# Scratch of a weight piece reused two loop steps later, threshold by TENSOR_REDUCE, first queries on ScalarE's queue, first raw weights asked for inside the loop

## The chip, the core and the metric

The kernel runs on one core of a Trainium2 chip. The time is device microseconds of one execution. The three timed runs of the kernel before gave 985.11, 971.95 and 981.6 us, median 981.6. The profile was taken in a further execution of 973.75 us, whose span, from the first to the last instruction, is 972.0 us.

## The reference

Four batches, 576 positions, 8 heads of 64 columns, all in fp32 (the weights come as 64-bit floats). The reference computes, cut to what matters:

```python
scores = scale * q @ k.T                          # per batch and head, 576 x 576
thresh = max(scores, axis=-1) - tau
scores = where(scores >= thresh, scores, -1e9)
attn   = softmax(scores);  x = attn @ v           # heads side by side: 4 x 576 x 512
u  = x + real(fft(fft(x, axis=1), axis=2))        # Fourier mixing over positions and columns
un = (u - mean(u)) / sqrt(var(u) + 1e-6)
x  = u + relu(un @ w_ch1) @ w_ch2                 # 512 -> 2048 -> 512
gate = sigmoid(causal depthwise convolution of x over 5 positions, conv_w)
out  = (gate * (x @ w_val)) @ w_out
```

Each query row keeps only the scores within tau of its maximum.

## The kernel before

The program has one instruction stream for each engine, written out in the order in which Python emits it; no scheduler reorders it. It has two halves.

**The attention loop** (`attention_fft`). The 32 heads are taken in 16 pairs. A pair has 9 score tiles (four 128-row tiles for each head, and one that joins the last 64 rows of both), so there are 144 tiles, two to a loop step: 72 steps and a few more to drain. `ORDER` is a string of atoms that sets what a step emits. `M0`, `M1` (line 570) take the negative row maxima of the two tiles into `neg`, 128x2; `TH` (line 573) makes the threshold `thr` out of them, one instruction of VectorE for both tiles; `E0`, `E1` (line 577) are ScalarE's exponentials, with `neg` as bias; `K0`, `K1` (line 587) mask the exponentials with `thr` and sum them; `C` and `R` make the reciprocal of the sum, `N0`, `N1` (line 594) scale the rows on GpSimd (POOL), `T0`, `T1` transpose them on TensorE, `S2`, `S3` (line 559) are the score products of the next step's tiles. There are two PSUM buffers of scores, so the products of a next tile wait for the mask of a tile before. Between the atoms a filler emits products of probabilities and values (line 304), transposes of the next pair's keys and queries (244 to 263), and the Fourier products (line 228).

Keys, queries and values come by DMAs on SyncE's queue (SP): `load_qk` asks for keys (`kn`, line 186), the last 32 keys and 64 queries (`tn`, 187 and 189) and the other queries (`qn`, 192). Once a batch, a piece of the Fourier stage is written to DRAM in reverse order, element by element, by a DMA on SP (line 356).

**Weight pieces.** The weights come as 64-bit words. 32 pieces of the first two weight matrices, and 8 of the last two, are each converted by a list of instructions in `Wide.stages` (lines 96 to 106): seven or eight on VectorE, ScalarE and, last, POOL. A piece needs a buffer of raw words, filled by a DMA on POOL's queue (`load_raw`, line 866), and one of two pairs of scratch tiles, `cx` and `ct`. In the attention loop the atoms `WD`, `WA` and `WP` each emit at most one instruction of a piece, for VectorE, ScalarE or POOL. `tick` runs at the end of each step: it counts the step, stores the high and low half of a finished piece to DRAM (`e_h<-cx`, `e_l<-ct`, line 919, on SP), puts its scratch pair on the list `stored` with the step from which it may be taken again (the present one and `STORE` more, here 0), and asks for new raw words. The first instruction of a piece (line 96) writes `cx`, and so waits on the chip until the store that last read this scratch has landed. In the loop 18 pieces are converted.

**The second half** (`mlp`, `gate_out`): the drain of the attention, norms, the two large products (lines 1054 and 1070), the gate and the last two products. It begins with DMAs that fetch the stored pieces (line 849, first at 426.8 us).

Of the kernel before, what the change touches and what calls it, by code (L numbers as in the profile page):

```python
# [11 lines left out]
F32 = mybir.dt.float32  # L12
# [3 lines left out]
AF = mybir.ActivationFunctionType  # L16
ALU = mybir.AluOpType
AX = mybir.AxisListType
# [3 lines left out]
B, H, S, D = 4, 8, 576, 64  # L22
# [4 lines left out]
MAIN, TAIL = 512, 64  # L27
HALF = S // 2
# [12 lines left out]
SPLITS = 6  # L41
KEYS_ACT = False
CYCLE = 'wfgssvgwnsfhtc'
STORE = 0
SPENT = 2
EARLY = 18
QORD = (1, 0, 4, 2, 3)
# [8 lines left out]
def f32(ap):  # L56
    return ap.bitcast(F32)
# [77 lines left out]
def attention_fft(tc, right, ps_f, a, u_d, dram, conv_w, hooks):  # L135
    nc = tc.nc
    PE, DVE, ACT, POOL, SP = nc.tensor, nc.vector, nc.scalar, nc.gpsimd, nc.sync
    left, right1 = ExitStack(), ExitStack()
    with ExitStack() as right2, ExitStack() as right2b, ExitStack() as right3, ExitStack() as right4, ExitStack() as scores, ExitStack() as turned:
        def pool(stack, name, bufs, side="right", **kw):  # L140
            return stack.enter_context(tc.tile_pool(name=name, bufs=bufs, side=side, **kw))
# [3 lines left out]
        const = pool(right1, "const", 1)  # L145
        x_p = pool(right1, "x", XB)
        sm_p = pool(right1, "sm", 6)
# [10 lines left out]

        ident = id_p.tile([128, 128], F32, name="ident")
        tau = const.tile([128, 1], F32, name="tau_sb")  # L160
        ntau = const.tile([128, 1], F32, name="ntau")
        alpha = const.tile([128, 1], F32, name="alpha")
        cst = {}
        POOL.dma_start(out=tau, in_=a["tau"].to_broadcast([128, 1]))
        hooks["begin"]()
        DVE.memset(alpha, 0.0)
        ACT.activation(ntau, alpha, AF.Exp)

        vs = [(const.tile([128, 2, 4, D], F32, name=f"v{i}"), const.tile([128, 2, D], F32, name=f"vt{i}")) for i in range(2)]
        ths = [[const.tile([128, 2, n], F32, name=f"th{i}_{n}") for n in (256, 320)] for i in range(2)]  # L170
# [5 lines left out]
        NPAIR = B * NP  # L176
        nat = {}

        def load_qk(p):
            b, hs = p // NP, slice(2 * (p % NP), 2 * (p % NP) + 2)  # L180
            kn = nat_p.tile([128, 2, 2, 2, D], F32, tag="kn", name="kn")
            qn = nat_p.tile([128, 2, 4, 2, D], F32, tag="qn", name="qn")
            tn = nat_p.tile([96, 2, 2, D], F32, tag="tn", name="tn")
            k, q = a["k"][b, hs].rearrange("h (g p) d -> p h g d", g=2), a["q"][b, hs]
            for j in range(2):
                SP.dma_start(out=kn[:, j], in_=k[j * 128:j * 128 + 128])
            SP.dma_start(out=tn[0:32], in_=k[256:HALF])
            for j in range(2):
                SP.dma_start(out=tn[32:96, :, j], in_=q[:, MAIN:S].rearrange("h p d -> p h d"))
            for h in range(2):  # L190
                for j in range(2):
                    SP.dma_start(out=qn[:, h, :, j], in_=q[h, 0:MAIN].rearrange("(t p) d -> p t d", p=128))
            nat[p] = tn, kn, qn

        def load_v(p):
# [37 lines left out]
        def g_prep_qk(p):  # L233
# [33 lines left out]
            if 0 < p < NPAIR - 1:  # L267
                load_qk(p + 1)
# [271 lines left out]
        sc, neg, thr, ex, ssum, prob = {}, {}, {}, {}, {}, {}  # L540
# [24 lines left out]

        def emit_max(g):
            if g % 2 == 0:
                neg[g // 2], thr[g // 2], ssum[g // 2] = (sm_p.tile([128, 2], F32, tag=nm, name=nm) for nm in ("neg", "thr", "su"))
            i, j = divmod(g, 2)
            DVE.tensor_reduce(out=neg[i][:, j:j + 1], in_=sc[g][:, :, 0:HALF], axis=AX.XY, op=ALU.max, negate=True)  # L570

        def emit_thr(i):
            DVE.tensor_scalar(out=thr[i], in0=neg[i], scalar1=-1.0, scalar2=ntau[:, 0:1], op0=ALU.mult, op1=ALU.add)

        def emit_exp(g):
            e = e_p.tile([128, 2, HALF], F32, tag="e", name="e")
            ACT.activation(e, sc[g][:, :, 0:HALF], AF.Exp, bias=neg[g // 2][:, g % 2:g % 2 + 1], scale=1.0)  # L577
            ex[g] = e

        def emit_mask(g):  # L580
# [38 lines left out]
        def emit_t(g):  # L619
# [20 lines left out]
            if h == 2:  # L640
                q_tail.append(g_tail(p, c, [p_t[p, i][:, MAIN:S]], th[0:64, :, 256:320], (i,)))

        LAG = 4
        SP.dma_start(out=ident, in_=a["ident"])
        load_qk(0)
        DVE.tensor_scalar(out=ntau, in0=tau, scalar1=-1.0, scalar2=None, op0=ALU.mult)
        DVE.tensor_tensor(out=ntau, in0=ntau, in1=tau, op=ALU.min)
        DVE.tensor_scalar(out=alpha, in0=tau, scalar1=0.0, scalar2=float(D) ** -0.5,
                          op0=ALU.is_ge, op1=ALU.mult)
        q_prep.append(g_prep_qk(0))  # L650
        while q_prep:
            fill(1e9)
            flush()
        load_qk(1)
        emit_s(0)
        emit_s(1)
# [8 lines left out]
        for u in range(NT // 2 + 3):  # L665
            t = 2 * u
            on = [x for x in (t, t + 1) if x < NT]
            state["tile"] = t
            for x in on:
                p, h, i = tiles[x]  # L670
# [7 lines left out]
            on2 = bool(on)  # L678
# [3 lines left out]
            def M0():  # L682
                if on2: emit_max(t)
            def M1():
                if on2: emit_max(t + 1)
            def TH():
                if on2: emit_thr(u)
            def E0():
                if on2: emit_exp(t)
# [21 lines left out]
                if t + 3 < NT: emit_s(t + 3)  # L711
            def C():
                if on2: ACT.activation(ssum[u], ssum[u], AF.Copy, bias=1e-9)
            def TA():
                if on2: ACT.activation(thr[u], neg[u], AF.Identity, scale=-1.0, bias=ntau[:, 0:1])
            def TP():
                if on2: POOL.tensor_scalar(out=thr[u], in0=neg[u], scalar1=-1.0, scalar2=ntau[:, 0:1], op0=ALU.mult, op1=ALU.add)
            def CP():
                if on2: POOL.tensor_scalar(out=ssum[u], in0=ssum[u], scalar1=1e-9, scalar2=0.0, op0=ALU.add, op1=ALU.add)
            def Q():  # L720
# [22 lines left out]
            for atom in ORDER.split():  # L743
                env[atom]()
            tq.clear()
            hooks["tick"]()
            if left and NPAIR - 1 in kq:
                left.close()
# [33 lines left out]
def mlp(tc, right, ps_f, attention, hooks, a, u_d, y_d, dram, wide, cw, out):  # L782
    nc = tc.nc
    PE, DVE, ACT, POOL, SP = nc.tensor, nc.vector, nc.scalar, nc.gpsimd, nc.sync
# [6 lines left out]
    with ExitStack() as ctx, ExitStack() as top, ExitStack() as top2:  # L791
# [16 lines left out]
        active, outbox, stored = deque(), [], deque()  # L808
        at, loaded, clock = [0], [0], [0]
# [19 lines left out]
        def give(slot):  # L829

            if nxt[0] < FB:
                nxt[0] += 1
                assign(nxt[0] - 1, slot)
            else:
                assign(gone.pop(0), slot)
# [10 lines left out]
        def place(k):  # L846
            j, i = pieces[k][1]
            for t, d in zip(w[j][i], e_d[k]):
                SP.dma_start(out=f32(t), in_=d)
            placed.add(k)  # L850
# [56 lines left out]
        def tick():  # L907

            clock[0] += 1
            while spent and spent[0][0] <= clock[0]:  # L910
                nxt[1] -= 1
                give(spent.popleft()[1])
            while stored and stored[0][0] <= clock[0]:
                spare["cv"].append(stored.popleft()[1])
            for k, room, dst in outbox:
                j, i = pieces[k][1]
                if isinstance(j, str) or k < EARLY:
                    for t, d in zip(dst, e_d[k] if k < EARLY else [d[i * 128:(i + 1) * 128] for d in w_d[j]]):
                        SP.dma_start(out=d, in_=f32(t))
                    written.add(k)  # L920
                    if k in wanted:
                        place(k)
                else:
                    placed.add(k)
                stored.append((clock[0] + STORE, room))
                spare["raw"].append(raws.pop(k)[0])
            outbox.clear()
            load_raw()
# [188 lines left out]
        tail = None  # L1117
# [413 lines left out]
```

## Time and profile before

| | |
|---|---|
| timed runs | 985.11, 971.95, 981.6 us (median 981.6) |
| profiled execution | 973.75 us, span 972.0 us, mean granted TensorE clock 0.978 |
| PE (TensorE products) | busy 894.6 us, 92% |
| DVE (VectorE) | busy 580.0 us, 60% |
| ACT (ScalarE) | busy 454.2 us, 47% |
| POOL (GpSimd) | busy 368.0 us, 38% |

Shares over the whole span mix two halves: up to about 425 us TensorE and VectorE are both busy most of the time and wait for each other; from about 450 us on TensorE is busy all of it but for a stretch around 525 to 545 us. A row of the timeline gives the start, the duration, the engine, the line and the instruction; what stands in square brackets is how long the engine had been idle before it, and what ended that. An engine name with a q (SPq) is the queue on which a DMA is issued, and the duration is that of issuing it.

### The profile page before, as it was taken

What the parts mean: (1) busy time and instruction counts of PE and PEld (TensorE: products, weight loads), DVE (VectorE), ACT (ScalarE), POOL (GpSimd) and SP (SyncE); (2) the same over time, 40 slices, a digit from 0 to 9 for tenths busy, and PEclk for the clock granted to TensorE, in tenths of its full rate; (3) what the DMA queues carried; (4) which work ended last, traced back from release to release, by engine and by line L of the source; (5) the groups of instructions that cost most, each with busy time, mean ns of one, the idle gap of its engine ahead of it and who ended that gap; (6) DMA issues with size and microseconds to landing.
All of it is one profiled execution on the core that took longest, in us unless ns stands there. A gap on an engine that the chain in (4) does not pass through costs nothing. (4 is left out here: it accounts for less than half of the span.)

```text
span 972.0 us, 14884 instructions
## 1 busy us (share of the span) xinstructions
PE 894.6 (92%) x5232; PEld 712.3 (73%) x5232; DVE 580.0 (60%) x1228; ACT 454.2 (47%) x915; POOL 368.0 (38%) x450
## 2 busy tenths in 40 slices
PE   4888986898979999979997999999999999999998
PEld 2555564555756566648885899999999989998897
DVE  4998876787968677732569534444222256734750
ACT  3767764666767676643545423322312213214432
POOL 2475542476627634561455412321031011028421
PEclk9999897998999999999999999999999999999999
DMA  7686441465637442257637922421230022143211
GB/s 182 155 198 155 137 118 66 141 171 168 166 111 203 131 108 80 78 186 286 232 112 250 345 107 87 135 69 42 71 114 1 1 88 86 44 143 109 102 44 66
DMA packets 136227, 123.61 MB, mean 127 GB/s; under 512 B 86630, under 2 KB 100182, under 8 KB 136152
## 3 DMA queue, kind: packets, MB, share of 16 engines
q1 hardware_dynamic: 129160, 98.16, 33.0%
q0 software_dynamic: 6992, 24.49, 8.4%
q8 instruction: 42, 0.69, 0.3%
q14 instruction: 33, 0.27, 0.1%
HBM read 90.11 MB, written 37.22 MB: 131 GB/s over the span
## 5 line engine op out<-in xcount | busy, mean ns | idle before, releaser
L1058 DVE SCALAR_TENSOR_TENSOR hl<-h,hh 128x448 fp32r<-128x448 f32 (+1 forms) x80 | 50.9, 637 | 203.5 <-ACT hh L1057 203.5
L1057 ACT ACTIVATE hh<-h 128x448 fp32r<-128x448 f32 (+1 forms) x80 | 44.4, 555 | 257.7 <-PE h L1054 257.7
L594 POOL TENSOR_SCALAR p<-p,su 128x576 f32<-128x576 f32 x144 | 109.1, 763 | 125.1 <-DVE su L681 103.9
L559 PE MATMUL s<-kt,qt 64*128 64x288 f32 (+1 forms) x640 | 105.9, 467 | 30.2 <-DVE p L587 30.0
L587 DVE SCALAR_TENSOR_TENSOR p<-s,thr,e 128x576 f32<-128x576 f32 x144 | 112.5, 815 | 34.0 <-ACT e L577 16.3
L1070 PE MATMUL c<-hl,w1h 128*128 128x448 f32 (+1 forms) x320 | 118.9, 371 | 0.5 <-DVE hl L1058 0.5
L1070 PE MATMUL c<-hh,w1h 128*128 128x448 f32 (+1 forms) x320 | 119.0, 372 | 0.0
L1070 PE MATMUL c<-hh,w1l 128*128 128x448 f32 (+1 forms) x320 | 118.7, 371 | 0.0
L577 ACT ACTIVATE e<-s,neg 128x576 f32<-128x576 f32 x144 | 99.4, 736 | 41.2 <-DVE neg L570 41.0
L570 DVE TENSOR_REDUCE neg<-s 128x1 f32<-128x576 f32 x144 | 101.7, 745 | 15.5 <-PE s L559 15.2
L559 PEld LDWEIGHTS s<-kt,qt 64*128 64x128 f32 (+1 forms) x640 | 47.2, 184 | 74.4 <-DVE p L587 27.9
L637 ACT ACTIVATE m<-t 128x512 f32<-128x512 f32 x144 | 84.5, 587 | 7.7 <-PE t L628 7.7
L1054 PE MATMUL h<-unh,w0h 128*128 128x448 f32 (+1 forms) x320 | 80.2, 372 | 5.4 <-DMA w0h<-e_h 3.2
L1054 PE MATMUL h<-unh,w0l 128*128 128x448 f32 (+1 forms) x320 | 80.9, 375 | 4.2 <-POOL w0l L106 4.2
L628 PE MATMUL t<-ident,p 128*128 128x128 f32 x576 | 79.3, 281 | 3.7 <-POOL xf L334 1.9
L304 PE MATMUL f<-m,v 128*64 128x320 f32 (+1 forms) x512 | 80.4, 415 | 1.7 <-ACT m L637 1.2
L1054 PE MATMUL h<-unl,w0h 128*128 128x448 f32 (+1 forms) x320 | 80.7, 374 | 0.0
L628 PEld LDWEIGHTS t<-ident,p 128*128 128x128 f32 x576 | 65.4, 143 | 19.7 <-issue 9.9
L1054 PEld LDWEIGHTS h<-unh,w0h 128*128 128x128 f32 x320 | 59.9, 188 | 13.4 <-DMA w0h<-e_h 3.8
L1054 PEld LDWEIGHTS h<-unh,w0l 128*128 128x128 f32 x320 | 60.1, 189 | 12.1 <-POOL w0l L106 5.5
L1054 PEld LDWEIGHTS h<-unl,w0h 128*128 128x128 f32 x320 | 60.7, 190 | 7.0
L1070 PEld LDWEIGHTS c<-hl,w1h 128*128 128x128 f32 x320 | 60.1, 188 | 7.7 <-DVE hl L1058 0.8
(218 smaller groups left out, 1574.5 us busy)
## 6 DMA issues: line engine op xcount, KB each, us to landing
raw<-in_moe_w_ch POOLq DMA_DIRECT2D x32, 512.0 KB, 5.5
qn<-in_q SPq DMA_DIRECT2D x64, 128.0 KB
e_h<-cx SPq DMA_DIRECT2D x18, 256.0 KB
e_l<-ct SPq DMA_DIRECT2D x18, 256.0 KB
xs<-xt SPq DMA_DIRECT2D x16, 288.0 KB
w0h<-e_h SPq DMA_DIRECT2D x18, 256.0 KB
w0l<-e_l SPq DMA_DIRECT2D x18, 256.0 KB
w1h<-e_h SPq DMA_DIRECT2D x18, 256.0 KB
```

What stands on the lines that cost most here:

```text
L304: PE.matmul(out=f[h * 64:h * 64 + 64, 0:n], lhsT=w, rhs=r, start=(t == 0), stop=(t == 4))
L559: PE.matmul(out=s[o, c, 0:HALF], lhsT=qt[w, hh, q], rhs=kt[w, hh, :], start=True, stop=True)
L570: DVE.tensor_reduce(out=neg[i][:, j:j + 1], in_=sc[g][:, :, 0:HALF], axis=AX.XY, op=ALU.max, negate=True)
L577: ACT.activation(e, sc[g][:, :, 0:HALF], AF.Exp, bias=neg[g // 2][:, g % 2:g % 2 + 1], scale=1.0)
L587: DVE.scalar_tensor_tensor(out=p_view(g).rearrange("p (a b) -> p a b", a=2), in0=sc.pop(g)[:, :, 0:HALF], scalar=thr[g // 2][:, j], in1=ex ...
L594: POOL.tensor_scalar(out=v, in0=v, scalar1=su, scalar2=1.0, op0=ALU.mult, op1=ALU.mult)
L628: PE.matmul(out=f[:, t, :], lhsT=pv[:, t * 128:(t + 1) * 128], rhs=ident, is_transpose=True, start=(t == 0), stop=(t == 3))
L637: tq.append(lambda: ACT.activation(o, fv, AF.Copy))
L1054: PE.matmul(out=f[:, 0:n], lhsT=ww[:, k * 128:(k + 1) * 128], rhs=x[:, k, 0:n], start=(i == 0), stop=(i == 3 * KB - 1))
L1057: ACT.activation(hh, f[:, 0:n], AF.Relu)
L1058: DVE.scalar_tensor_tensor(out=hl, in0=f[:, 0:n], scalar=0.0, in1=f32(hh), op0=ALU.max, op1=ALU.subtract)
L1070: PE.matmul(out=ch[c][o][:, 0:n], lhsT=ww[:, o * 128:(o + 1) * 128], rhs=x, start=(at_ == 0 and i == 0), stop=(at_ == FB - 1 and i == 2))
```

## The change

Four things. The scratch of a finished piece goes back on the list with `STORE = 2`, so that the next piece may take it two loop steps later; in the second half it stays 0. The threshold is one TENSOR_REDUCE with negation over pairs (negative maximum, `atau`), in six fixed tiles `neg0` to `neg5` whose second column is filled with `atau`, the larger of tau and minus tau, by twelve copies at the start; before it was one TENSOR_SCALAR. The load of tau, and the query loads of the first pair, are issued by ScalarE instead of POOL and SP. And the call that first asks for raw weights is taken from the start of the kernel and put at the end of the second loop step.

```diff
-STORE = 0
+STORE = 2
...
-        ntau = const.tile([128, 1], F32, name="ntau")
+        atau = const.tile([128, 1], F32, name="atau")
...
-        POOL.dma_start(out=tau, in_=a["tau"].to_broadcast([128, 1]))
-        hooks["begin"]()
+        negs = [const.tile([128, 2, 2], F32, name=f"neg{i}") for i in range(6)]
+        ACT.dma_start(out=tau, in_=a["tau"].to_broadcast([128, 1]))
         DVE.memset(alpha, 0.0)
-        ACT.activation(ntau, alpha, AF.Exp)
+        ACT.activation(atau, alpha, AF.Exp)
...
-        def load_qk(p):
+        def load_qk(p, second=SP):
...
-                SP.dma_start(out=tn[32:96, :, j], in_=q[:, MAIN:S].rearrange("h p d -> p h d"))
+                second.dma_start(out=tn[32:96, :, j], in_=q[:, MAIN:S].rearrange("h p d -> p h d"))
...
-                    SP.dma_start(out=qn[:, h, :, j], in_=q[h, 0:MAIN].rearrange("(t p) d -> p t d", p=128))
+                    second.dma_start(out=qn[:, h, :, j], in_=q[h, 0:MAIN].rearrange("(t p) d -> p t d", p=128))
...
-            DVE.tensor_reduce(out=neg[i][:, j:j + 1], in_=sc[g][:, :, 0:HALF], axis=AX.XY, op=ALU.max, negate=True)
+            DVE.tensor_reduce(out=neg[i][:, j, 0:1], in_=sc[g][:, :, 0:HALF], axis=AX.XY, op=ALU.max, negate=True)
 
         def emit_thr(i):
-            DVE.tensor_scalar(out=thr[i], in0=neg[i], scalar1=-1.0, scalar2=ntau[:, 0:1], op0=ALU.mult, op1=ALU.add)
+            DVE.tensor_reduce(out=thr[i], in_=neg[i], axis=AX.X, op=ALU.add, negate=True)
...
-        load_qk(0)
-        DVE.tensor_scalar(out=ntau, in0=tau, scalar1=-1.0, scalar2=None, op0=ALU.mult)
-        DVE.tensor_tensor(out=ntau, in0=ntau, in1=tau, op=ALU.min)
+        load_qk(0, ACT)
+        DVE.tensor_scalar(out=atau, in0=tau, scalar1=-1.0, scalar2=None, op0=ALU.mult)
+        DVE.tensor_tensor(out=atau, in0=atau, in1=tau, op=ALU.max)
+        for t in negs:
+            for j in range(2):
+                DVE.tensor_copy(t[:, j, 1:2], atau)
...
             tq.clear()
+            if u == 1:
+                hooks["begin"]()
             hooks["tick"]()
...
-                stored.append((clock[0] + STORE, room))
+                stored.append((clock[0] + (STORE if tail is None else 0), room))
```

`hooks["begin"]` is `load_raw`, which `tick` calls too, at its own end. TensorE's order stays the same, row for row; so does every engine's order from the end of the attention loop on. What moves in the loop is the pieces. On VectorE, at the place where the first batch's Fourier products begin (step 24; `ael` and `aeh` are parts of their result, `su` the row sums), the kernel before has the end of one piece (101, 102) and straight behind it the first instruction of another (96):

```order
L389 TENSOR_TENSOR ael<-f,aeh 97x258 [waits Activation_49]
L101 SCALAR_TENSOR_TENSOR raw<-raw,ct 128x512
L102 TENSOR_SCALAR raw<-cx 128x512
L96 TENSOR_SCALAR cx<-raw 128x512 [waits DMAHW2_49,DMASW1_49]
L681 RECIPROCAL su<-su 128x2 [waits Activation_49]
L570 TENSOR_REDUCE neg<-s 128x1 [waits PE_49] x2
L389 TENSOR_TENSOR ael<-f,aeh 96x258 [waits Activation_49]
L573 TENSOR_SCALAR thr<-neg,ntau 128x2 [waits DVE_49]
```

In the changed kernel the same place has the middle of a piece (100), and the first instruction of the next one a step later:

```order
L389 TENSOR_TENSOR ael<-f,aeh 97x258 [waits Activation_49]
L100 SCALAR_TENSOR_TENSOR cx<-raw,cx 128x512
L685 RECIPROCAL su<-su 128x2 [waits Activation_49]
L571 TENSOR_REDUCE neg_189<-s 128x1 [waits PE_49] x2
L389 TENSOR_TENSOR ael<-f,aeh 96x258 [waits Activation_49]
L574 TENSOR_REDUCE thr<-neg_189 128x2 [waits DVE_49]
L588 SCALAR_TENSOR_TENSOR p,su<-s,thr,e 128x576 [waits DVE_49,Activation_49]
L588 SCALAR_TENSOR_TENSOR p,su<-s,thr,e 128x576 [waits Activation_49,Pool_49]
L389 TENSOR_TENSOR ael<-f,aeh 96x258 [waits Activation_49]
L101 SCALAR_TENSOR_TENSOR raw<-raw,ct 128x512
L102 TENSOR_SCALAR raw<-cx 128x512
L96 TENSOR_SCALAR cx<-raw 128x512 [waits DMAHW6_49,DMASW7_49]
```

From here on the changed kernel begins a piece every third step, and the last instructions of the eighteenth (101, 102) stand in step 58 of 72; before, in step 51, with up to six instructions of pieces in one step on VectorE and none in others. The scratch that a piece takes was stored about three steps before.

The other place is the start. On POOL's queue the kernel before has tau, then three loads of raw words, then the first row scaling:

```order
L164 DMA tau_sb_185<-in_tau 128x1
L866 DMA raw_189<-in_moe_w_ch1 128x4x256
L866 DMA raw_191<-in_moe_w_ch2 128x1024
L866 DMA raw_193<-in_moe_w_ch1 128x4x256
L594 ISA
L594 TENSOR_SCALAR p_292<-p_292,su_274 128x576 [waits DVE_49]
```

In the changed kernel:

```order
L868 DMA raw_326<-in_moe_w_ch1 128x4x256
L868 DMA raw_328<-in_moe_w_ch2 128x1024
L868 DMA raw_330<-in_moe_w_ch1 128x4x256
L595 ISA
L595 TENSOR_SCALAR p_303<-p_303,su_285 128x576 [waits DVE_49]
```

The three loads still stand ahead of everything else that POOL does, and none of them waits for anything; only tau is gone. ScalarE's stream of the changed kernel begins with tau, the table load, and the six query loads, of which the last three wait for earlier DMAs (`DMAHW4_49` is the semaphore of the first of the two `tn` loads in front of them):

```order
L165 DMA tau_sb<-in_tau 128x1
L167 ACT_TABLE_LOAD
L167 ACTIVATE atau<-alpha 128x1 [waits DVE_49]
L189 DMA tn<-in_q 64x2x64 x2
L192 DMA qn<-in_q 128x4x64
L192 DMA qn<-in_q 128x4x64 [waits DMAHW0_49]
L192 DMA qn<-in_q 128x4x64 [waits DMAHW2_49]
L192 DMA qn<-in_q 128x4x64 [waits DMAHW4_49]
L257 ACTIVATE qt<-f,alpha 128x2x64 [waits DVE_49,PE_49]
```

Before, that stream went from the table load and one ACTIVATE straight to line 257, and the six loads stood on SP behind `ident`, two `kn` and one `tn`.

## Rows read from the trace of the kernel before

**Rows 1.** Page, part 1: busy us, share of the span, instructions.
```profile
PE 894.6 (92%) x5232; PEld 712.3 (73%) x5232; DVE 580.0 (60%) x1228; ACT 454.2 (47%) x915; POOL 368.0 (38%) x450
```

**Rows 2.** Windows: stretch, its length, busy of each engine, TensorE clock, DMA share, GB/s.
```profile
150.00:175.00 25.00, 17.15 (x117) 12.66 (x119) 20.04 (x47) 14.88 (x32) 7.54 (x10) 0.84 0.19 59
...
200.00:225.00 25.00, 23.93 (x163) 14.17 (x160) 20.96 (x45) 15.28 (x32) 18.92 (x24) 1.00 0.75 198
```

**Rows 3.** Waits, all engines: who waited for whom, us in total, times, longest.
```profile
PE s L559 <- DVE p L587: 30.0, 29, 3.0
...
DVE cx L96 <- DMA e_h<-cx: 16.8, 3, 10.9
DVE p L587 <- ACT e L577: 16.3, 18, 2.3
```

**Rows 4.** Timeline, step 24: reversal, piece's store, VectorE's and TensorE's idle time.
```profile
133.01 0.69 SPq L356 DMA_DIRECT2D xr<-xs  x1
...
133.81 9.59 SPq L919 DMA_DIRECT2D e_h<-cx  x1
...
151.54 0.43 DVE L96 TENSOR_SCALAR cx<-raw 128x512 int32<-128x512 int32 x1 [10.95 <-DMA e_h<-cx]
...
153.75 1.17 PE L228 MATMUL f<-sdh,xoh 128*96 128x256 f32 x4 [9.69 <-DVE ael L389]
```

**Rows 5.** Timeline, 262 to 286 us: the second such wait.
```profile
273.37 0.43 DVE L96 TENSOR_SCALAR cx<-raw 128x512 int32<-128x512 int32 x1 [4.46 <-DMA e_h<-cx]
...
275.57 0.39 PE L254 MATMUL f<-ident,tn 96*128 96x96 f32 x2 [3.36 <-DVE bol L389]
```

**Rows 6.** Lines of VectorE, 0 to 440 us: count, busy us, mean ns, idle before.
```profile
L573 DVE TENSOR_SCALAR thr<-neg,ntau 128x2 f32<-128x2 f32 x72 | 31.5, 438 | 2.0
...
L97 DVE TENSOR_SCALAR ct<-raw 128x512 int32<-128x512 int32 x18 | 12.1, 671 | 0.0
```

**Rows 7.** Single lines: count, duration ns least/median/most, first and last start.
```profile
L573 DVE TENSOR_SCALAR thr<-neg,ntau x72: 216/266/1906, 16.7 to 419.2; 128x2 f32<-128x2 f32 x72
...
L570 DVE TENSOR_REDUCE neg<-s x144: 725/746/760, 15.0 to 418.4; 128x1 f32<-128x576 f32 x144
...
L681 DVE RECIPROCAL su<-su x72: 145/157/171, 19.3 to 423.6; 128x2 f32<-128x2 f32 x72
...
L97 DVE TENSOR_SCALAR ct<-raw x40: 406/420/3497, 36.0 to 664.6; 128x512 int32<-128x512 int32 x40
```

**Rows 8.** Timeline, step 24: a long threshold beside POOL, and who waits.
```profile
135.74 1.91 DVE L573 TENSOR_SCALAR thr<-neg,ntau 128x2 f32<-128x2 f32 x1
136.16 1.47 POOL L594 TENSOR_SCALAR p<-p,su 128x576 f32<-128x576 f32 x2
...
138.63 1.49 PE L559 MATMUL s<-kt,qt 64*128 64x288 f32 x8 [1.41 <-DVE p L587]
```

**Rows 9.** Timeline, first 16 us: loads, and TensorE's and VectorE's first waits.
```profile
0.74 1.28 ACT L167 ACT_TABLE_LOAD   x1 [0.74 <-PEq L1520]
...
1.24 0.74 POOL L164 DMA_DIRECT2D tau_sb<-in_tau  x1 [0.80 <-POOLq L1520]
...
1.97 2.05 POOL L866 DMA_DIRECT2D raw<-in_moe_w_ch  x3
...
2.74 1.39 SPq L189 DMA_DIRECT2D tn<-in_q  x2
...
4.18 2.61 SPq L192 DMA_DIRECT2D qn<-in_q  x4
...
10.43 0.56 PE L254 MATMUL f<-ident,tn 96*128 96x96 f32 x2 [4.41 <-DMA tn<-in_q]
...
14.98 0.76 DVE L570 TENSOR_REDUCE neg<-s 128x1 f32<-128x576 f32 x1 [3.33 <-PE s L559]
```

**Rows 10.** Tile e_h: stores and later fetches, count, duration ns, first and last start.
```profile
L919 SPq DMA_DIRECT2D e_h<-cx x18: 319/430/9591, 45.5 to 312.4; - x18
L849 SPq DMA_DIRECT2D w0h<-e_h x18: 319/320/9483, 426.8 to 547.1; - x18
```

More of the change, by code (lines that the diff above doesn't have):

```diff
@@ L567, in emit_max @@
             if g % 2 == 0:
-                neg[g // 2], thr[g // 2], ssum[g // 2] = (sm_p.tile([128, 2], F32, tag=nm, name=nm) for nm in ("neg", "thr", "su"))
+                thr[g // 2], ssum[g // 2] = (sm_p.tile([128, 2], F32, tag=nm, name=nm) for nm in ("thr", "su"))
+            neg[g // 2] = negs[g // 2 % len(negs)]
             i, j = divmod(g, 2)
-            DVE.tensor_reduce(out=neg[i][:, j:j + 1], in_=sc[g][:, :, 0:HALF], axis=AX.XY, op=ALU.max, negate=True)
+            DVE.tensor_reduce(out=neg[i][:, j, 0:1], in_=sc[g][:, :, 0:HALF], axis=AX.XY, op=ALU.max, negate=True)
         def emit_thr(i):
-            DVE.tensor_scalar(out=thr[i], in0=neg[i], scalar1=-1.0, scalar2=ntau[:, 0:1], op0=ALU.mult, op1=ALU.add)
+            DVE.tensor_reduce(out=thr[i], in_=neg[i], axis=AX.X, op=ALU.add, negate=True)
         def emit_exp(g):
             e = e_p.tile([128, 2, HALF], F32, tag="e", name="e")
-            ACT.activation(e, sc[g][:, :, 0:HALF], AF.Exp, bias=neg[g // 2][:, g % 2:g % 2 + 1], scale=1.0)
+            ACT.activation(e, sc[g][:, :, 0:HALF], AF.Exp, bias=neg[g // 2][:, g % 2, 0:1], scale=1.0)
             ex[g] = e
@@ L713, in C @@
                 if on2: ACT.activation(ssum[u], ssum[u], AF.Copy, bias=1e-9)
[L714 to L717, printed above, removed]
             def CP():
```

## The prediction

> **What bounds the kernel now.** I read the page's shares first [rows 1]. TensorE's 92% says little, since it mixes two halves; so next the windows of 25 us. In the second half TensorE works without a break, and the change leaves every engine's order there as it is. The attention loop is another matter: from 200 to 225 us TensorE is busy 23.93 us and VectorE 20.96; from 150 to 175 us TensorE has only 17.15 at a granted clock of 0.84, VectorE 20.04 [rows 2]. Both are nearly full and wait for each other, by the two score buffers: products, maxima, threshold, masks, next products. Any time by which the masks come sooner can move the loop, and any stop of VectorE stops TensorE a little later.
>
> Then the waits [rows 3]. The products of a next tile waited 30.0 us, 29 times, for a mask. VectorE waited 16.8 us, in three pieces of up to 10.9, for the store of a piece's high half: it stood at the first instruction of a piece (line 96), whose scratch was still being read, with maxima and masks queued behind. Last the places. At step 24 the reversal goes out on SP at 133.01; the store behind it takes 9.59 us to issue, and VectorE starts again at 151.54, idle for 10.95 us; TensorE starts at 153.75 after 9.69 idle [rows 4]. At 273.37 the same costs VectorE 4.46 and TensorE 3.36 [rows 5]. The third piece of the wait, 16.8 less these two, is 1.4 us.
>
> The other loss is line 573, the threshold. Its 72 instructions take 31.5 us, 438 ns in the mean [rows 6], but the shortest takes 216 ns and the longest 1906 [rows 7]. At 135.74 it lasts 1.91 us and ends when POOL's two row scalings end (136.16 + 1.47 = 137.63); TensorE then waits 1.41 us for the mask [rows 8]. An instruction on 128x2 numbers has no work for that: it is held while POOL works.
>
> **The scratch.** A step takes (419.2 - 16.7) / 71 = 5.67 us, from the first and last threshold [rows 7], so two steps are 11.3 us. The longest wait is 10.95, so the added distance covers each of the three. At step 24 there is also no first instruction of a piece behind the reversal any more: it stands a step later, on scratch stored about three steps before, 17.0 us, against 151.54 - 133.81 = 17.7 from that store's issue to VectorE's release in the worst case [rows 4]. I take the two gaps of TensorE, 9.69 + 3.36 = 13.0 us, as the gain. Ends: nothing, if another wait ends as late; 16.8 us, all that VectorE stood.
>
> What that costs: each piece comes later, the last in step 58 instead of 51. Seven steps are 40 us; the last store now goes out at 312.4, then at about 352, and the first fetch comes at 426.8 [rows 10]. Hidden by 74 us; without that margin the excess would come in full. Instructions of pieces stay the same in number, about 90 on VectorE, and lie more evenly: nothing for that.
>
> **The threshold.** Held time is 31.5 - 72 x 0.216 = 15.9 us. How much of it reaches the end? In 18 steps the mask waited for the exponentials anyway, 16.3 us in all [rows 3], and there a shorter threshold is worth nothing; where it lasted longest, TensorE lost 1.41 of the 1.69 us above the shortest [rows 8]. So at most 54 of 72 steps times 83%, 62%; I take half, 8 us, if TENSOR_REDUCE isn't held. Does a row say so? The 144 maxima, the same operation, stay between 725 and 760 ns, but read PSUM; the reciprocals of 128x2, SBUF to SBUF, between 145 and 171; TENSOR_SCALAR from SBUF goes to 3497 ns (line 97) [rows 7]. That is for it, not proof. The Trainium skill (SBUF — State Buffer, section "SBUF: two separate sides") says that VectorE and GpSimd lock one shared pair of ports against each other for a whole instruction, and that VectorE needs it for two-port modes or two SBUF inputs; the Trainium skill's page VectorE: DVE Perf Modes, section "The perf-mode tier table", gives tensor_reduce no two-port mode. By that rule it is never held; the trace agrees on who is held, and no run here shows the new instruction.
>
> Its own length: the nearest row in size is the reciprocal of 128x2, median 157 ns. From above: the maximum's 745 ns for 576 numbers, shrunk as TENSOR_SCALAR shrinks from 128x512 to 128x2 (least 406 to 216 ns [rows 7]), is 0.40 us. I take 157, since four numbers are nearest to two: 72 x 0.059 = 4.2 us less on VectorE, half of it on the path, 2 us. At 0.40 it costs 72 x 0.184 = 13.2 us and eats nearly all of the 15.9.
>
> **The start.** The diff says that raw words are asked for later. The order says that they are not: nothing stands ahead of the three loads on POOL, and they wait for nothing, so they go out when POOL starts, at 1.24 instead of 1.97, with tau's 0.74 us gone [rows 9]. What held the first queries back should thus stay: they were issued from 2.74 on, and TensorE got them at 10.43, having waited 4.41 us. ScalarE can't issue them sooner than SP did: behind tau stands its table load, 0.74 to 2.02. Issuing takes ScalarE 1.39 + 2.61 = 4.0 us [rows 9], at a time when it has nothing else to do; were it busy, 4.0 us. The twelve copies, 12 x 0.157 = 1.9 us, lie in a VectorE that later idles 3.33 us for the first scores. I take 0. Ends: a gain of 4.41, the whole wait; a loss where the last query load waits for the first `tn`, as its semaphore now says: issued at 10.43 and landing as `tn` did, 7.69 us after its issue, it is there at 18.1, and the first maximum, with 1.49 us for the products [rows 8], starts at 19.6 instead of 14.98, 4.6 later.
>
> **Sum.** 13 + 8 + 2 + 0 = 23 us, against the profiled execution of 973.75: 951 us. That execution lies 7.85 us under the median of 981.6, and the three runs span 13 us. I put the median two thirds of that distance above the sum: **956 us**.
>
> **Rivals.**
> 1. TENSOR_REDUCE is held or slow as well, and only the scratch gains. For it: no row has this operation on SBUF operands alone; against it the reciprocals. 973.75 - 13 = 961, median 966. The Trainium skill speaks for this too: its page VectorE: DVE Perf Modes, section "Rules for kernel authors", calls tensor_reduce on a hot path VectorE's slowest operation, at 1×; at twice the 216 ns the sum would lose 72 x 0.216 = 15.6 us of VectorE's 15.9, and come to the same 961. The row on the maxima fits 1×, but here there are four elements. Chance 0.13.
> 2. The wait for a store comes back: a piece now begins every third step whatever the queue does, and a store that goes out behind a reversal needs 17.7 us against 17.0. Only the threshold's 10 us are left: 964, median 969. Against it: at step 24 no such instruction stands there any more. Chance 0.13.
> 3. The raw words do come later after all: the 4.41 us at the start are gained as well. 947, median 952. Against it the order. Chance 0.05.
> 4. Slower: the time for which POOL holds VectorE moves to the pieces' own instructions, which now stand singly in nearly every step beside the row scalings. Line 97 already takes 671 ns in the mean, 265 above its least [rows 6, 7]. If each of 90 instructions waited for one scaling, 0.73 us, that is 66 us on VectorE, half of it, 33, on the path: 973.75 - 23 + 33 = 984, median 989. It decides from 0.51 us on each, twice what line 97 has. Chance 0.05.
> 5. TensorE fills the time: its gaps come back elsewhere, the sum stays within 5 us of 974. Chance 0.07.
>
> The forecast, with both gains between half and full, has 0.57: 938 to 965.
>
> **Range and chances.** About 2% is what a measurement of this kernel can tell from no change; 2% below 981.6 is 962. The range runs from 938 (16.8, 15.9 and 4.2 us in full, 973.75 - 37, with little added) to 974, which takes in rivals 1 to 3. Faster by over 2%: three quarters of the forecast, rival 3 and a little of 1 and 2, 0.54. Slower by over 2%, beyond 1001, needs more than rival 4 at its price: 0.04. Within 2%: 0.42.
>
> **What will show it.** Line 96 has no wait for `e_h`, and TensorE no gap above 5 us between 130 and 160 us. The threshold's 72 rows lie near 160 ns, the longest under 250, about 12 us in all. TensorE's wait for masks falls from 30.0 to under 20 us. Raw loads stand at about 1.2 us, and the first maximum within 4 us of 14.98. The first fetch of a stored piece moves from 426.8 to about 404, and everything behind it by as much. I am wrong if the threshold still spreads to above 1 us, if line 96 still waits, or if both are as forecast and 426.8 hardly moves.

## The result, and the profile after

The changed kernel takes 943.96 us in the median (940.76 to 945.86) against 980.86 in runs of the kernel before beside it: a ratio of 0.963, 95% interval 0.956 to 0.971. On a second chip it took 943.1 against 976.0, ratio 0.967 (0.964 to 0.969). The prediction of 956 us, with a range of 938 to 974, called it faster; it fell 12 us short of the gain. The profiled execution took 940.76 us, span 939.0.

The page's first part, busy us, share and instructions, answers [rows 1]:

```profile
PE 882.5 (94%) x5232; PEld 705.2 (75%) x5232; DVE 561.6 (60%) x1240; ACT 453.0 (48%) x915; POOL 365.0 (39%) x449
```

TensorE does the same 5232 products in 12.1 us less busy time. That is the first thing that the prediction had no term for. The windows of 25 us [rows 2] show where:

```profile
150.00:175.00 25.00, 23.20 (x174) 15.57 (x172) 20.77 (x51) 19.73 (x44) 13.65 (x20) 1.00 0.56 160
200.00:225.00 25.00, 23.41 (x176) 14.63 (x176) 21.46 (x51) 20.15 (x44) 15.35 (x22) 1.00 0.63 181
```

The stretch that had 17.15 us of TensorE at a granted clock of 0.84 has 23.20 at 1.00. Over the whole loop, from the first threshold to the last, the same view of the kernel before and, after it, of the changed kernel on the second chip:

```profile
17.00:419.00 402.00, 352.79 (x2478) 231.78 (x2476) 319.51 (x730) 270.14 (x572) 209.89 (x280) 0.95 0.50 137
```
```profile
17.00:388.00 371.00, 341.90 (x2479) 226.94 (x2477) 304.09 (x731) 268.73 (x572) 206.38 (x280) 0.99 0.54 148
```

31 us go. 10.9 of them are TensorE's busy time, at a mean granted clock of 0.99 instead of 0.95; 20.1 are its idle time. I sorted that idle time by the length of the gaps between one product's end and the next one's start: gaps above 2 us fall from 23.5 us in six places to 2.5 in one, and those of 0.5 to 2 us stay (22.9 and 24.1 us). So the gain is long stops and what follows them, not a little from every step. The waits say the same [rows 3]. First a line of that view of the kernel before which is not among those rows, then the changed kernel's:

```profile
ACT e L577 <- DVE neg L570: 41.0, 29, 10.6
```
```profile
PE s L559 <- DVE p L588: 27.1, 29, 2.5
ACT e L578 <- DVE neg L571: 25.8, 23, 2.9
DVE p L588 <- ACT e L578: 14.4, 24, 1.3
```

TensorE's many short waits for masks hardly change (30.0 before); ScalarE's waits for the maxima lose 15.2 us, and the one of 10.6 is gone. No wait of line 96 for a store is left. The reversal and the store behind it still go out, and that store still takes 7.67 us to issue; nothing on VectorE waits for it, and the next piece begins at 137.73 without a wait [rows 4]:

```profile
131.05 0.69 SPq L356 DMA_DIRECT2D xr<-xs  x1
...
132.29 7.67 SPq L921 DMA_DIRECT2D e_h<-cx  x1
...
137.73 0.42 DVE L96 TENSOR_SCALAR cx<-raw 128x512 int32<-128x512 int32 x1
```

The single lines [rows 7], duration least/median/most in ns:

```profile
L574 DVE TENSOR_REDUCE thr<-neg x72: 141/157/159, 17.0 to 385.5; 128x2 f32<-128x4 f32 x72
...
L571 DVE TENSOR_REDUCE neg<-s x144: 730/747/759, 15.5 to 384.7; 128x1 f32<-128x576 f32 x144
...
L97 DVE TENSOR_SCALAR ct<-raw x40: 408/422/4112, 39.7 to 631.4; 128x512 int32<-128x512 int32 x40
```

The new threshold is never held. Line 97 still is, and now more: 921 ns in the mean over the loop, before 671 [rows 6]:

```profile
L97 DVE TENSOR_SCALAR ct<-raw 128x512 int32<-128x512 int32 x18 | 16.6, 921 | 0.0
```

The start [rows 9]:

```profile
1.26 2.26 POOL L868 DMA_DIRECT2D raw<-in_moe_w_ch  x3 [0.81 <-POOLq L1522]
...
1.43 1.32 ACTq L189 DMA_DIRECT2D tn<-in_q  x2
...
10.50 0.90 PE L244 MATMUL f<-ident,kn 128*128 128x128 f32 x3 [5.25 <-DMA kn<-in_k]
...
15.54 1.42 DVE L571 TENSOR_REDUCE neg<-s 128x1 f32<-128x576 f32 x2 [2.63 <-PE s L559]
```

The raw loads go out at 1.26, as the order said. The queries are no longer what TensorE waits for; now it is the second half of the keys, at 10.50. The first maximum starts 0.56 us later than before.

The fetches of the stored pieces [rows 10] begin 33.5 us earlier, and what is behind them keeps that distance to within 1 us:

```profile
L921 SPq DMA_DIRECT2D e_h<-cx x18: 376/422/7932, 51.9 to 315.4; - x18
L851 SPq DMA_DIRECT2D w0h<-e_h x18: 319/320/9062, 393.3 to 513.3; - x18
```

### The profile page after: what moved, and what is told of

Its sections match the earlier page's. It is cut to its first block, busy times and chain, and to the rows that moved or that the text cites. A ratio compares the mean times of both kernels' runs of the same rounds, so it can differ in the third digit from the quotient of the medians.

```text
span 939.0 us, 14896 instructions
## 1 busy us (share of the span) xinstructions
PE 882.5 (94%) x5232; PEld 705.2 (75%) x5232; DVE 561.6 (60%) x1240; ACT 453.0 (48%) x915; POOL 365.0 (39%) x449
## 5 line engine op out<-in xcount | busy, mean ns | idle before, releaser
L559 PE MATMUL s<-kt,qt 64*128 64x288 f32 (+1 forms) x640 | 99.6, 441 | 27.1 <-DVE p L588 27.1
L559 PEld LDWEIGHTS s<-kt,qt 64*128 64x128 f32 (+1 forms) x640 | 45.2, 175 | 69.0 <-issue 27.8
L1056 PEld LDWEIGHTS h<-unh,w0h 128*128 128x128 f32 x320 | 60.1, 189 | 11.4 <-ACT w0h L105 3.0
L106 POOL TENSOR_TENSOR ct<-raw 128x512 fp32r<-128x512 f32 x26 | 28.8, 1113 | 99.5 <-DVE raw L102 55.0
## 6 DMA issues: line engine op xcount, KB each, us to landing
w0h<-e_h SPq DMA_DIRECT2D x18, 256.0 KB, 16.1
```

The costliest lines, as they stand in the source:

```text
L559: PE.matmul(out=s[o, c, 0:HALF], lhsT=qt[w, hh, q], rhs=kt[w, hh, :], start=True, stop=True)
L1056: PE.matmul(out=f[:, 0:n], lhsT=ww[:, k * 128:(k + 1) * 128], rhs=x[:, k, 0:n], start=(i == 0), stop=(i == 3 * KB - 1))
```

## The experiments

**Theory A**: the gain is the two terms of the prediction, each enlarged by what follows a stop of VectorE: TensorE stands, its granted clock falls, and the next products are slower. **Rival B**: the terms are only mis-sized (the stops' own length, the threshold's held time in full). Each kernel was timed over five rounds beside the kernel before; gains are given in per cent of it (1% is 9.8 us), with 95% intervals. Experiments 1 to 4 ran on one chip; 6, 9, 10 and the changed kernel on a second; 5, 7, 8 and 11 on a third. Across chips, "by the ratios" compares the gains over the kernel before, "by the medians" the times as they are.

**1. Without the scratch's distance.**

```diff
-STORE = 2
+STORE = 0
```

> The changed kernel with STORE = 0, all else as changed: a finished piece's scratch is free for the next piece at once, so line 96 should stand behind the store again. Theory A (what the long stops cost is TensorE's idle time and also the lower granted clock behind them; the scratch is worth about 24 us, 16 of stops and 8 of slower products): 943.96 + 24 = 968 us, line 96 waits about 17 us for stores, TensorE's granted clock in the loop falls below 0.97 in the stretches behind the stops. Rival B (the scratch is worth its stops alone, as predicted, and the threshold nearly all its held time): 943.96 + 14 = 958 us.

961.7 us, a gain of 1.6% (1.3 to 1.9) instead of the changed kernel's 3.3: the distance is worth 1.7%, 16.7 us. The wait is back, but shorter than before, 6.02 us, because in this kernel the pieces begin a step later than in the kernel before; TensorE then waits 4.94 us:

```profile
151.27 0.43 DVE L96 TENSOR_SCALAR cx<-raw 128x512 int32<-128x512 int32 x1 [6.02 <-DMA e_h<-cx]
...
153.47 1.06 PE L609 MATMUL f<-ident,p 128*64 128x128 f32 x4 [4.94 <-DVE thr L574]
```

A's 24 us is out. Rival B's 14 lies at the edge of the interval (13 to 20 us), but the wait is only a third of the one that B priced, so something beside the stop seems to be in it (experiment 5).

**2. Without TENSOR_REDUCE.**

```diff
-            DVE.tensor_reduce(out=thr[i], in_=neg[i], axis=AX.X, op=ALU.add, negate=True)
+            DVE.tensor_scalar(out=thr[i], in0=neg[i][:, :, 0], scalar1=-1.0, scalar2=atau[:, 0:1], op0=ALU.mult, op1=ALU.subtract)
```

> The changed kernel with the threshold by TENSOR_SCALAR as before (negated and less atau, out of the same six tiles), all else as changed. Theory A: the threshold is worth about 10 us as predicted: 954 us; its 72 rows take about 31 us again, the longest near 1.9 us. Rival B (threshold in VectorE's chain is worth nearly all of its 20 us, and more by the clock): 964 us. Rival C (TENSOR_REDUCE's gain is given back elsewhere, the scratch is all of it): 944 to 946 us.

960.0 us, a gain of 1.8% (1.4 to 2.1): here the threshold is worth 1.6%, 15.4 us, between A and B. The line in this kernel:

```profile
L574 DVE TENSOR_SCALAR thr<-neg,atau x72: 215/322/5567, 17.4 to 408.9; 128x2 f32<-128x2 f32 x72
```

Two of its instructions take 5.57 us each, beside the same sequence of POOL's instructions. The timeline of the first place, in which POOL's rows are those to look at, and behind it the second instruction:

```profile
181.14 5.57 DVE L574 TENSOR_SCALAR thr<-neg,atau 128x2 f32<-128x2 f32 x1
181.53 0.81 POOL L332 TENSOR_TENSOR xf<-xt 128x287 f32<-128x287 f32 x1
182.31 0.74 POOL L595 TENSOR_SCALAR p<-p,su 128x576 f32<-128x576 f32 x1
183.03 0.78 POOL L448 TENSOR_TENSOR xr<-xr,sm 128x289 f32<-128x289 f32 x1
183.77 0.78 POOL L341 TENSOR_TENSOR xel<-xf,xeh 128x289 fp32r<-128x289 f32 x1
184.54 0.73 POOL L595 TENSOR_SCALAR p<-p,su 128x576 f32<-128x576 f32 x1
185.25 0.68 POOL L450 TENSOR_TENSOR xr<-xr,dd 128x287 f32<-128x287 f32 x1
185.90 0.78 POOL L341 TENSOR_TENSOR xol<-xf,xoh 128x287 fp32r<-128x287 f32 x1
...
187.69 2.29 PE L559 MATMUL s<-kt,qt 64*128 64x288 f32 x8 [4.96 <-DVE p L588]
...
286.41 5.57 DVE L574 TENSOR_SCALAR thr<-neg,atau 128x2 f32<-128x2 f32 x1
```

Seven instructions of POOL follow each other without a break, the threshold ends 0.03 us after the last, and TensorE stood for 4.96 us. All 72 thresholds take 45.1 us in this execution, against 31.5 before, and most of the growth is in these two. The execution took 966.87 us, the longest of this kernel's six; how often the two are met in the others isn't shown.

**3. The scratch alone**, on the kernel before.

```diff
-STORE = 0
+STORE = 2
...
-                stored.append((clock[0] + STORE, room))
+                stored.append((clock[0] + (STORE if tail is None else 0), room))
```

> The kernel before with STORE = 2 in the loop and nothing else of the change. Theory A: 980.9 - 24 = 957 us, no wait of line 96 for a store, threshold still 31 us in all. Rival B: 980.9 - 14 = 967 us. If a store stands again where a piece begins every third step: within 4 us of 980.

959.6 us, 1.65% (1.25 to 2.05) or 16.1 us: A's 24 was too much, B's 14 lies within the interval. No wait for a store is left. The thresholds, still TENSOR_SCALAR, take 35.1 us in all, against 31.5 before; here none is held as long as in experiment 2:

```profile
L573 DVE TENSOR_SCALAR thr<-neg,ntau x72: 215/284/2144, 17.3 to 406.0; 128x2 f32<-128x2 f32 x72
```

**4. TENSOR_REDUCE alone**, on the kernel before, with its six tiles and twelve copies.

```diff
...
-            DVE.tensor_scalar(out=thr[i], in0=neg[i], scalar1=-1.0, scalar2=ntau[:, 0:1], op0=ALU.mult, op1=ALU.add)
+            DVE.tensor_reduce(out=thr[i], in_=neg[i], axis=AX.X, op=ALU.add, negate=True)
...
```

> The kernel before with the threshold by TENSOR_REDUCE over pairs and the twelve copies, nothing else of the change. Theory A: 980.9 - 10 = 971 us, thresholds about 11 us in all, line 96 still waiting about 17 us for stores. Rival B: 961 us. Rival C: 979 to 981 us.

966.1 us, 1.0% (0.7 to 1.4) or 10.1 us, the prediction's term, and nearer to it than the interval of 6.5 to 13.6 us can tell; rival B's 20 is out. The wait for stores stays, with its longest piece at the old place:

```profile
149.57 0.43 DVE L96 TENSOR_SCALAR cx<-raw 128x512 int32<-128x512 int32 x1 [12.56 <-DMA e_h<-cx]
```

**5. Half the distance.**

```diff
-STORE = 2
+STORE = 1
```

> The changed kernel with STORE = 1: one loop step of 5.1 us between a store and the next use of its scratch. Theory A (the distance must cover the store that goes out behind the reversal, up to 17.7 us from issue to landing): line 96 waits again near step 25 or 26, up to 6 us, and with the lower clock behind it the time is 947 to 952 us. Rival B (it is enough that the piece no longer begins in the step of the reversal): no wait, within 2 us of 943.

961.85 us, 1.6% (1.3 to 1.85): as slow as with STORE = 0, and outside both expectations. The one wait, 6.09 us, is as A had it, but the loop is 15.3 us longer than the changed kernel's, and only 7.8 of that lies in the three steps of the stop. A reason can be read from the order: with 1 the pieces' instructions stand in the very steps where they stand with 0, and from one threshold to the next VectorE has up to three of them, often twice in a row; with 2 it is three, one, one, over and over from about step 14 on. (More than three in a step, as stood above under the change, is not possible: `ORDER` has three atoms `WD`, and the traces show at most three.) Of the other 7.5 us 1.4 come in the first three steps, ahead of every piece, where experiment 6's kernel loses as much against the same trace; 3.7 come between the steps 9 and 12, and there experiment 1's kernel, with the same order, loses as much. There, in the kernel with 1 and then in the changed one:

```profile
60.62 1.40 DVE L101 SCALAR_TENSOR_TENSOR raw<-raw,ct 128x512 f32<-128x512 uint32 x1
...
61.94 0.42 DVE L102 TENSOR_SCALAR raw<-cx 128x512 int32<-128x512 int32 x1
62.27 1.90 DVE L96 TENSOR_SCALAR cx<-raw 128x512 int32<-128x512 int32 x1
...
66.77 2.29 PE L559 MATMUL s<-kt,qt 64*128 64x288 f32 x8 [2.64 <-DVE p L588]
```
```profile
59.07 1.40 DVE L101 SCALAR_TENSOR_TENSOR raw<-raw,ct 128x512 f32<-128x512 uint32 x1
60.39 0.42 DVE L102 TENSOR_SCALAR raw<-cx 128x512 int32<-128x512 int32 x1
...
64.26 1.50 PE L559 MATMUL s<-kt,qt 64*128 64x288 f32 x8 [0.87 <-DVE p L588]
64.86 0.48 DVE L96 TENSOR_SCALAR cx<-raw 128x512 int32<-128x512 int32 x1
```

In the first, 101, 102 and the next piece's 96 stand together, 3.7 us of VectorE ahead of a maximum, of which 96 alone, 0.42 us in the median, took 1.90; TensorE loses 2.64 us at the next products, in the second 0.87. The windows from 60 to 76 us, in the same order of kernels:

```profile
60.00:76.00 16.00, 12.76 (x73) 7.49 (x71) 11.73 (x24) 9.19 (x20) 9.78 (x14) 0.79 0.77 182
```
```profile
60.00:76.00 16.00, 15.13 (x107) 9.79 (x108) 11.69 (x30) 10.90 (x23) 10.18 (x13) 0.94 0.84 192
```

A granted clock of 0.79 instead of 0.94, and 73 products instead of 107 with VectorE equally busy. So part of what the distance gives seems to be that pieces are spread. I have no kernel that spreads them without lengthening the distance; that some 6 us belong to the spreading is read from these steps, not shown by a run of its own.

**6. One stop, put in.** Eight maxima over a constant, with an unused result, at the end of step 24.

```diff
...
+            if u in (24,):
+                for _ in range(8):
+                    DVE.tensor_reduce(out=idle, in_=f32(cst["cdh"]), axis=AX.XY, op=ALU.max)
```

> The changed kernel, with eight maxima over the constant cdh (128x1032 each, result unused) on VectorE at the end of step 24: one stop of about 10.7 us (8 x 1.33, by size from the maxima of 576 numbers) where the kernel before stood for 10.95 us. Theory A (a stop costs TensorE's gap of some 9.5 us and then slower products while the granted clock is at its lower level, 3 to 6 us more): 12 to 16 us slower than the changed kernel. Rival B (the stop costs its gap alone): 9 to 10.5 us. Rival C (the loop's waits elsewhere absorb part of it): under 8 us.

```profile
L748 DVE TENSOR_REDUCE idle<-cdh x8: 1219/1228/1228, 134.3 to 143.1; 128x1 f32<-128x1032 f32 x8
```
```profile
146.69 1.17 PE L229 MATMUL f<-sdh,xoh 128*96 128x256 f32 x4 [8.01 <-DVE ael L390]
```
```profile
140.00:153.00 13.00, 6.31 (x31) 4.41 (x32) 11.47 (x22) 3.57 (x8) 4.35 (x6) 0.61 0.22 75
```
```profile
146.70:152.40 5.70, 5.70 (x26) 3.80 (x27) 4.56 (x12) 2.01 (x6) 2.28 (x3) 0.50 0.18 64
```

954.5 us, 11.4 more than the changed kernel by the medians, 11.0 by the ratios. The stop was 9.8 us long, shorter than planned, TensorE stood 8.01, and the steps 24 to 27 took 10.8 us more; from there on the two kernels run step for step alike. So 2.8 us beyond the gap were paid. The last window shows where: from the end of the gap to 152.40 TensorE was busy all the time, at a granted clock of 0.50, so at 1.2 GHz instead of 2.4, and what it did in these 5.70 us would have taken half as long at 2.4, an estimate of 2.85 us. A's mechanism, below its size; rival B, at this gap alone, would have been 8, and the runs of the two kernels, on one chip, lie 9 to 14 us apart (95% interval).

**7. The same work in four stops** of 2.46 us, in the steps 14, 24, 34 and 44 (the edit is against experiment 6's kernel).

```diff
-            if u in (24,):
-                for _ in range(8):
+            if u in (14, 24, 34, 44):
+                for _ in range(2):
```

> The changed kernel with the same eight maxima over cdh as in the kernel with one stop, but two at the end of each of the steps 14, 24, 34 and 44: 2.46 us of VectorE four times, 9.8 us in all as there. Theory A (a short stop costs TensorE less than its length, by the slack in its waits, and brings little or none of the lower clock): 4 to 8 us slower than the changed kernel at 943, against 11.4 us for the one stop. Rival B (the length counts, however it is cut): 9 to 10 us slower. Rival C (each short stop brings its own stretch at the lower clock): 11 us or more slower.

951.9 us: 8.8 more by the medians, 7.7 by the ratios; a microsecond of VectorE costs 0.8 to 0.9 here, 1.1 in the one stop. Theory A's upper end, and not far from B. Round the second and the third stop the granted clock stayed at 1.00 (130 to 160 and 188 to 205 us); behind the first and the fourth it was 0.79 (87 to 95) and 0.72 (250 to 256).

**8. Every threshold twice**: 72 times 0.157 us, in all 11.4 us.

```diff
             DVE.tensor_reduce(out=thr[i], in_=neg[i], axis=AX.X, op=ALU.add, negate=True)
+            DVE.tensor_reduce(out=thr[i], in_=neg[i], axis=AX.X, op=ALU.add, negate=True)
```

> The changed kernel with each threshold computed twice into the same tile: 72 x 0.157 = 11.3 us more on VectorE, none of it held while POOL works. Theory A (about half of what VectorE does between maxima and masks lies on the path, the share that the prediction took): 5 to 7 us slower than 943. Rival B (VectorE's chain is the loop: all of it): 10 to 12 us. Rival C (evenly spread small work disappears in the waits for ScalarE's exponentials): under 3 us.

947.0 us, 3.9 more by the medians, 3.1 by the ratios (by their intervals from nothing to 7): between A and C, about 0.3 us for each microsecond. With the two kernels above this makes a series: the same 10 to 11 us of VectorE cost 3 to 4 us in 72 pieces, 8 to 9 in four, 11 in one.

**9. The start undone**, the pieces kept in their steps (the raw words count as loaded at the first step's end).

```diff
...
-        ACT.dma_start(out=tau, in_=a["tau"].to_broadcast([128, 1]))
+        POOL.dma_start(out=tau, in_=a["tau"].to_broadcast([128, 1]))
+        hooks["begin"]()
...
-        load_qk(0, ACT)
+        load_qk(0)
...
-            if u == 1:
-                hooks["begin"]()
...
-                raws[k] = room, room_pool.tile([128, 512, 2], I32, tag=tag, name="raw", bufs=1), clock[0]
+                raws[k] = room, room_pool.tile([128, 512, 2], I32, tag=tag, name="raw", bufs=1), max(1, clock[0])
```

> The changed kernel with its start undone: tau on POOL's queue, the first queries on SP behind the keys, the raw words asked for at the very start; every piece keeps its steps. Theory A (the start is worth nothing): within 1.5 us of the changed kernel, first maximum near 15 us. Rival B (it is worth the 4.4 us by which the kernel with STORE = 0 beats the kernel before with TENSOR_REDUCE alone, 966.1 - 961.7): 4 us slower.

942.5 us, 3.4% (3.2 to 3.65) against 3.3%: the new start is worth nothing. The 4.4 us between the kernels of experiments 1 and 4, which differ only in the start, go with the stop at the reversal, 6.02 us against 12.56, since the pieces stand a step apart there; no run takes the two apart. **The changed kernel itself** ran beside this one:

> The changed kernel itself, beside the three below on one chip. Expected 941 to 946 us, and as in its first profile no stretch of the loop at the lower granted clock, or at most two of 3.4 us.

943.1 us, as expected, with the lower clock in two places of the loop (0.51 from 24.5 to 28 and from 58.6 to 62 us). Its row of the loop is shown above.

**10. The raw loads really later.**

```diff
-            while spare["raw"] and loaded[0] < (len(pieces) if heads[1] == FB else 2 * FB):
+            while clock[0] >= 2 and spare["raw"] and loaded[0] < (len(pieces) if heads[1] == FB else 2 * FB):
...
-                raws[k] = room, room_pool.tile([128, 512, 2], I32, tag=tag, name="raw", bufs=1), clock[0]
+                raws[k] = room, room_pool.tile([128, 512, 2], I32, tag=tag, name="raw", bufs=1), clock[0] - (k < 3)
```

> The changed kernel, with the first three loads of raw words put behind the first two row scalings on POOL's queue, so that they really go out at about 20 us instead of 1.3; every piece keeps its steps. Theory A (three loads of 512 KB each keep the DMA engines busy until about 10 us, and the second load of keys lands at 10.5 because of them): keys land near 5 us, the first maximum starts at 11 to 12 us instead of 15.5, and the end comes 3 to 5 us sooner, 939 to 941 us. Rival B (the queries or another load land as late without them): within 1 us of the changed kernel. Rival C (the raw words now meet the first keys of the next pairs and the Fourier matrices): the start gains 4 us, the first pieces are late and give it back.

937.96 us (937.36 to 938.82), ratio to before 0.961 (0.959 to 0.963): 5.1 us better than the changed kernel on the same chip, the best version found. The start in its timeline:

```profile
2.79 2.54 ACTq L192 DMA_DIRECT2D qn<-in_q  x4
...
5.16 0.90 PE L244 MATMUL f<-ident,kn 128*128 128x128 f32 x3 [0.20 <-DMA kn<-in_k]
...
10.20 1.52 DVE L571 TENSOR_REDUCE neg<-s 128x1 f32<-128x576 f32 x2 [3.15 <-PE s L559]
...
15.90 2.27 POOL L868 DMA_DIRECT2D raw<-in_moe_w_ch  x3
```

Keys at 5.16 instead of 10.50, first maximum at 10.20 instead of 15.54; no piece is late for it. Rivals B and C are out.

**11. That kernel with the queries on SP** (the edit is against experiment 10's).

```diff
-        load_qk(0, ACT)
+        load_qk(0)
```

> The kernel with the raw loads really later, with the first pair's queries back on SP behind the keys. Theory A (the raw loads alone kept the queries late, the queue does not matter): first maximum within 1 us of 10.2 and time within 1 us of 938. Rival B (on SP the last query load is issued near 6.8 instead of 5.3 us and lands so much later): first maximum near 12 us, 939.5 to 940.

940.4 us, first maximum at 11.23, 1.03 us later than in experiment 10 and between the two expectations. By the medians, on two chips, ScalarE's queue is worth 2.5 us once the raw loads are out of the way, by the ratios 2.0, with an interval that takes in nothing; the 1.03 us at the first maximum are what the traces show. While the raw loads are in the way, the whole new start is worth nothing (experiment 9).

## Why the prediction was right, and where it failed

**The scratch: 13 us forecast, 16.1 alone and 16.7 in the changed kernel.** The stops went as described; line 96 waits no more. The 13 us lie within the interval of the first number (12 to 20) and at the edge of the second's, so the time alone doesn't show the term too small; the traces do. The step that failed is "lie more evenly: nothing for that", together with a price for the stops that ended with TensorE's gap. Neither what a stop leaves behind it (2.8 us beyond a gap of 8.01, shown by experiment 6) nor two crowded steps in a row (read from experiment 5) had a term. The row that could have told it was there: the granted clock of 0.84 from 150 to 175 us [rows 2] stood in the text, as a sign of trouble and not as a price.

**The threshold: 10 us forecast, 10.1 alone, 15.4 in the changed kernel.** The rows fell out as predicted: 157 ns, the longest 159, 11.1 us in all. The Trainium skill (SBUF — State Buffer, section "SBUF: two separate sides") says that VectorE and GpSimd lock the shared ports against each other for one instruction's length; the trace agrees on who is held, but the 5.57 us behind seven of POOL's instructions are more than one instruction's length. Half of what is saved as the part that counts was close: 10.1 us of 31.5 - 11.1 = 20.4. For time that isn't held it was too much: 0.3 (experiment 8). That the whole term came out to the microsecond is luck, by the width of its interval. And the failure here is the sum, which took the terms as if none knew of the others: how long a threshold is held depends on what POOL does beside it, and the scratch and the new start move VectorE's work against POOL's. With the scratch alone TENSOR_SCALAR's 31.5 us grow to 35.1 only (experiment 3); with the scratch and the start they grew to 45.1, two instructions of 5.57 us among them (experiment 2); whether the start alone does that, no run shows. The times don't carry this, since the intervals of 10.1 and 15.4 us overlap; the rows of the thresholds do, from one execution of each kernel.

**The start: 0 forecast, 0 measured**, and for the reason given: the loads go out as early as ever. That the wait would move to the second half of the keys was not foreseen. The ends were sound: the truly late loads gain 5.1 us, where rival 3 had 4.41.

**The sum.** By the ratios, the scratch alone 16.1 us (experiment 3), the threshold on top of it 15.4 (experiment 2), the start between them 1: 32.6 us, against 23 forecast. Of the 12 us between 956 and 943.96 these terms are about 10; the rest is the allowance of 5.2 for a median above its profiled execution, which was 3.2 for the changed kernel. Of the 31 us by which the loop is shorter a third, 10.9, is TensorE's busy time.

**The rivals.** 3 fell with the order of the start. 1 fell with the rows of line 574: on four numbers TENSOR_REDUCE takes 157 ns, where TENSOR_SCALAR on two took 216 at the least. The Trainium skill's page VectorE: DVE Perf Modes, section "Rules for kernel authors", which calls tensor_reduce the slowest operation, thus does not hold at this size; the measurement decides. 2 fell, since no wait for a store is left. 4 is there in small: line 97 is held for 921 - 671 = 0.25 us more on each of 18 instructions, 4.5 us of VectorE, where it decides from 0.51 on 90. 5 fell.

**What was to show it.** Right: no wait on line 96, no gap above 5 us between 130 and 160, the thresholds, raw loads at 1.26, first maximum 0.56 us from its old place. Wrong: TensorE's wait for masks fell from 30.0 only to 27.1 and not below 20, since the gain did not come out of the many short waits but out of the few long ones; and the first fetch came at 393.3, not 404, for the reasons above. The last store, put at about 352, went out at 315.4: the forecast moved it by seven steps, but took off nothing for the shorter steps ahead of it.

## What to carry to other kernels

In a loop where two engines wait for each other, price a stop by how it is cut: here 10 us of VectorE cost 3 to 4 us when spread over every step (by the interval, nothing to 7), 8 to 9 in four places and 11 in one; behind the one long stop TensorE's products ran at half the clock for 5.7 us. When one edit moves work to other steps, work out the other edits' terms again in the new steps: a held instruction costs what the other engine does at that moment. And where a diff says that a load comes later, read in the order what it waits for: these loads waited for nothing, and making them wait was worth 5 us more.

## What the runs showed of the hardware that I had not expected

An instruction of VectorE on 128x2 numbers was held for 5.57 us, twice in one execution, through seven instructions of POOL that followed each other, and went on only when POOL had a break. Three loads of raw words on POOL's queue, issued from 1.26 us on, held back a load of keys that SP had asked for at about the same time from 5.16 to 10.50 us. TensorE's granted clock lay at 0.79 over 16 us in which it was idle for 3.24 us in all (experiment 5), and at 1.00 in the changed kernel's profile from 150 to 175 us with 1.80 us idle. A copy of one column took 145 ns, and twelve in a row 0.82 us, not the 1.9 forecast, so that these small instructions overlap; the two thresholds of experiment 8, of which the second writes the same tile, did not.
